# The last two scores of an attention phase: each in a one-bank tile, copied out by VectorE and put under the wide exponential

## The chip, the cores and the metric

One core of a Trainium2 chip. TensorE (PE) multiplies, ScalarE (ACT) computes exponentials, VectorE (DVE) copies and adds, GpSimd (POOL) does small work, SyncE (SP) starts the transfers. The metric is the device time of one execution in microseconds; lower is better. Everything is float32, or float32 as the matmul's faster variant of it (fp32r).

## The reference

Two branches share the input x (2048 tokens, 512 channels) and are mixed by a gate per token. Branch a is softmax attention with 32 heads of 16 channels; branch b is a token-mixing MLP.

```
g = sigmoid((x * gate_w).sum(-1))
q, k, v = split((x @ wqkv), 32 heads of 16)
p = softmax(q k^T / 4);  a = (p v) @ wo
h = layernorm(x);  u = gelu(h^T w1 + b1);  b = (u w2 + b2)^T
out = g * a + (1 - g) * b
```

The exponentials of attention are 32 x 2048 x 2048 numbers. They are the subject of the change.

## The kernel before

**Stages.** Up to about 280 us the kernel loads x, computes the projections, the layer norm and the MLP's first layer. Then comes the attention stage: 128 *phases* in a row (the loop over `p`, 32 groups of two heads and half of the queries, four phases a group). After it, some 35 us of closing projections and stores.

**A phase.** Each phase makes 16 *scores*, numbered 0 to 15. A score is one matmul `kt` x `qt` into one PSUM bank, 128 keys x 512 queries (line 1025). It uses one half of PE's rows, and in the other half a matmul of the MLP's second layer or of a projection runs beside it (`dn`, line 1034; 14 or 12 of them a phase), so the last two or four scores of a phase go as pairs in the two halves. PSUM has eight banks: one is for `dn`, seven for the scores. Scores 0 to 6 take the seven banks; scores 7, 8, 9 reuse the banks of 0, 1, 2; from score 10 on, the banks are reused by tiles of two banks, `t`. Score 9's bank becomes `av` afterwards. The function `shares` says which bank is whose in each phase.

**The exponentials** go three ways, by the tables `EVAC`, `SINGLE` and `TWO`:

- scores 0, 2, 4, 6, 8, 9 (`SINGLE`): ACT takes each from its bank, 512 columns (line 1046);
- pairs (10, 11), (12, 13), (14, 15) (`TWO`): ACT takes two banks at once, 1024 columns (line 991, in `exps`);
- scores 1, 3, 5, 7 (`EVAC`): DVE copies each to the SBUF tile `pe` (line 1042), which frees the bank; when all four are there, ACT takes them at once and in place, 2048 columns (line 1057). Here this is called the *wide exponential*.

**After the scores**, `apply_v` multiplies the exponentials by v (line 921, 64 matmuls of a phase in the trace, four column groups side by side) into the bank `av`, and DVE adds that bank to the sum `ot` (line 943). The wide exponential comes last on ACT, so its scores are *held*: they are applied in the next phase, ahead of that phase's own. Before the change the pair (14, 15) is held with them.

**What sets the order.** The stage is recorded under a manual schedule: each engine runs its instructions in the order in which the code issues them. Waits are semaphores that an instruction raises when it is done. Two things in this order matter for what follows. On ACT a phase is six singles, three pairs, the wide exponential, and then the next phase's singles. And the wide exponential is given a wait beside the one for the copies, with the reason "a later instruction of this engine then waits for one engine alone": it waits for ACT's own instruction `pairs_done[1]`, the second pair of its phase.

```
for x in ([evac] if p < LAST else [evac[:, :2, :], evac[:, 2:, :]]):
    done = nc.scalar.activation(x, x, AF.Exp, scale=SCALE)
tc.add_manual_dep(done.ins, pairs_done[1].ins.name, SYNC, reason=EARLY)
```

On DVE a phase is four copies, then what the plan puts there (a tiny `mark`, casts of weights at line 67, in eight phases the five instructions of a late query projection, lines 67, 68 and 609 to 611), then the addition at line 943.

Of the kernel before, what the change touches and what calls it, by code (L numbers as in the profile page):

```python
# [9 lines left out]
F32 = mybir.dt.float32  # L10
# [13 lines left out]
P = 128  # L24
# [8 lines left out]
NB = 512  # L33
# [27 lines left out]
def gated_mix(ctx: ExitStack, tc: tile.TileContext, a_x, a_wqkv, a_wo, b_w1, b_b1, b_w2, b_b2, gate_w, out):  # L61
# [116 lines left out]
    with tc.tile_pool(name="vp", bufs=1, side="right") as pool:  # L178
# [15 lines left out]
        turns = {}  # L194
# [378 lines left out]
    LAST = NG * PHASES - 1  # L573
# [301 lines left out]

    token, mark = (out_pool.tile([1, 1], F32, name=name, bufs=1) for name in ("token", "mark"))

    EVAC = 1, 3, 5, 7
    SINGLE = 0, 2, 4, 6, 8, 9
    TWO = (10, 11), (12, 13), (14, 15)  # L880
    TURNS = [(0, 2), (4, 6), (8, 9), *TWO]
    HELD = [(1, 3), (5, 7)]

    def shares(n):

# [62 lines left out]
    with tc.manual_schedule(engines=engines):  # L948
        held, fence, turn, spare = [], None, 0, 0
        landed.clear()  # L950

        for p in range(LAST + 1):
            grp, ph = divmod(p, PHASES)
            second = ph % 2
            if ph == 0:
                sums[grp] = ot_pool.tile([P, NB], F32, name="ot")
                latest["clear"] = nc.gpsimd.memset(sums[grp], 0.0)
                at = [[0, 0], [0, 0]]
                if grp + 1 < NG:
                    qt[grp + 1] = load_q(grp + 1)  # L960
            if ph == 1 and grp + 1 < NG:
                kt[grp + 1] = load_k(grp + 1)
            for what, *args in calls.get(p, ()):
                what(*args)
            if not second:
                beside = [step(*args) for step, *args in dense.get(p // 2, ())]
            n_b = len(beside)
            half = slice(0, HALF) if second else slice(HALF, P)

            head = [second if n < n_b else (n - n_b + second * n_b) % 2 for n in range(NSC)]  # L970
            qbs = {}
            order = list(TURNS)
            if ph == 0 and n_b == NSC - 4:
                order[-2:] = (12, 14), (13, 15)
            for a, b in order + HELD:
                if head[a] == head[b]:
                    qbs[a], qbs[b] = 0, 1
                else:
                    zero, one = (a, b) if head[a] == 0 else (b, a)
                    qbs[zero], qbs[one] = turn, 1 - turn  # L980
                    turn = 1 - turn

            swap = ph == PHASES - 1 and p < LAST and n_b == NSC - 2
            if swap:
                order[-2:] = order[:-3:-1]

            def exps(n):
                pt = ptp.tile([P, 2, NB], F32, name="p2", bufs=len(TWO) + 1)
                where = [share[(j - BANKS) % BANKS] for j in (n - 1, n)]
                low = min(where)  # L990
                pairs_done.append(nc.scalar.activation(pt, twos[low, low + 1], AF.Exp, scale=SCALE))  # L991
                for j, k in zip((n - 1, n), where):
                    units[j] = *units[j][:3], pt[:, k - low, :]

            pairs_done = []
            evac = evp.tile([P, len(EVAC), NB], F32, name="pe")
            units = {}
            share = shares(spare)
            pool = regions()
            psum = pool.__enter__()  # L1000
            ones = [psum.tile([P, NB], F32, name=f"s{n}") for n in range(BANKS)]
            for n in range(NSC):
                i, qb = head[n], qbs[n]
                c = at[i][qb]
                at[i][qb] += 1
                if n < TWO[0][0]:
                    if n >= BANKS:
                        ones[share[n - BANKS]] = psum.tile([P, NB], F32, name=f"s{share[n - BANKS]}")
                    s = ones[share[n % BANKS]]
                else:  # L1010
                    if n == TWO[0][0]:
                        pool.__exit__(None, None, None)
                        pool = regions()
                        psum = pool.__enter__()
                        twos = {}
                        for low in range(BANKS):
                            if low == share[2]:
                                av = psum.tile([P, NB], F32, name="av")
                            elif low not in twos:
                                two = psum.tile([P, 2, NB], F32, name=f"t{low}")  # L1020
                                twos[low], twos[low + 1] = two[:, 0, :], two[:, 1, :]
                                twos[low, low + 1] = two
                    s = twos[share[(n - BANKS) % BANKS]]
                rows_i = slice(i * HALF, i * HALF + ROWS)
                nc.tensor.matmul(  # L1025
                    s,
                    kt[grp][rows_i, c * P : (c + 1) * P],
                    qt[grp][rows_i, qb * NB : (qb + 1) * NB],
                    start=True,
                    stop=True,  # L1030
                )
                if n < n_b:
                    ps, a, b, begin, last, done = beside[n]
                    mm = nc.tensor.matmul(ps, a[half], b[half], start=begin and not second, stop=last and bool(second))  # L1034
                    if n == 0 and fence is not None:
                        tc.add_manual_dep(mm.ins, fence.ins.name, SYNC, reason=REASON)
                    if n == n_b - 1:
                        fence = nc.gpsimd.memset(token, 0.0)  # L1038
                        tc.add_manual_dep(fence.ins, mm.ins.name, SYNC, reason=REASON)
                if n in EVAC:  # L1040
                    pt = evac[:, EVAC.index(n), :]
                    nc.vector.tensor_copy(pt, s)  # L1042
                    units[n] = i, c, qb, pt
                elif n in SINGLE:
                    pt = ptp.tile([P, NB], F32, name="p1", bufs=len(SINGLE))
                    nc.scalar.activation(pt, s, AF.Exp, scale=SCALE)  # L1046
                    units[n] = i, c, qb, pt
                else:
                    units[n] = i, c, qb, None
                    if n == TWO[0][1] or n == TWO[1][1] and not swap:  # L1050
                        exps(n)
                    elif n == TWO[2][1]:
                        exps(n)
                        if swap:
                            exps(TWO[1][1])
            for x in ([evac] if p < LAST else [evac[:, :2, :], evac[:, 2:, :]]):
                done = nc.scalar.activation(x, x, AF.Exp, scale=SCALE)  # L1057
            tc.add_manual_dep(done.ins, pairs_done[1].ins.name, SYNC, reason=EARLY)
            evac_done.append(done)
            if n_b and second and beside[-1][-1]:  # L1060
                beside[-1][-1]()
            if p == 0:
                shift_rows(nc.gpsimd, k_bufs[1])
            if p:
                met = nc.vector.memset(mark, 0.0)
                for before in (evac_done[-2], latest["add"], latest["clear"]):
                    tc.add_manual_dep(met.ins, before.ins.name, SYNC, reason=EARLY)
            if second:
                for _ in range(2):
                    if len(ready) < 2:  # L1070
                        split_weight(nc.vector.tensor_copy)
            for what, *args in later.get(p, ()):
                what(*args)

            turns, now_held = ([tuple(units[n] for n in pair) for pair in pairs] for pairs in (order, HELD))
            spare = share[2]
            if p < LAST:
                now_held = now_held + turns[-1:]
                turns = turns[:-1]
            if ph == 0:  # L1080
                if held:
                    apply_v(av, grp - 1, held, final=True)
                    spare = share[3]
                    av = twos[spare]
                apply_v(av, grp, turns)
            elif p < LAST:
                apply_v(av, grp, held + turns, await_loads=ph == PHASES - 1)
            else:
                ot = sums[grp]
                nc.vector.tensor_scalar_max(ot, ot, least[0])  # L1090
                apply_v(av, grp, held + turns + now_held, final=True)
                last_ot = ot
            pool.__exit__(None, None, None)
            held = now_held
            if ph == PHASES - 1:
                assert at == [[NS, NS], [NS, NS]]
# [166 lines left out]
```

## Time and profile before

| what | value |
|---|---|
| median of 3 runs | 1273.06 us (1272.27 to 1273.28) |
| the profiled execution, whole | 1273.23 us |
| its span, first to last instruction | 1271.4 us |
| DVE busy | 685.1 us, 54% of the span |
| POOL busy | 198.9 us, 16% |
| mean granted PE clock | 0.999 |
| first and last wide exponential | start at 284.4 and 1236.0 us |

The times below come from the one profiled execution, whose whole time lies 1.83 us above its span and 0.17 us above the median. In rows of the timeline the first number is the start in us from the start of the span, the second how long the row lasts from the first start to the last end; "x6" is six instructions that follow each other, whose times overlap.

### The profile page before, as it was taken

What the parts mean: (1) busy time and instruction counts of PE and PEld (TensorE: products, weight loads), DVE (VectorE), ACT (ScalarE), POOL (GpSimd) and SP (SyncE); (2) the same over time, 40 slices, a digit from 0 to 9 for tenths busy, and PEclk for the clock granted to TensorE, in tenths of its full rate; (3) what the DMA queues carried; (4) which work ended last, traced back from release to release, by engine and by line L of the source; (5) the groups of instructions that cost most, each with busy time, mean ns of one, the idle gap of its engine ahead of it and who ended that gap; (6) DMA issues with size and microseconds to landing.
All of it is one profiled execution on the core that took longest, in us unless ns stands there. A gap on an engine that the chain in (4) does not pass through costs nothing.

```text
span 1271.4 us, 32690 instructions
## 1 busy us (share of the span) xinstructions
PE 1263.2 (99%) x13342; PEld 827.5 (65%) x13342; DVE 685.1 (54%) x1282; ACT 1076.4 (85%) x1533; POOL 198.9 (16%) x316
## 2 busy tenths in 40 slices
PE   9999999999999999999999999999999999999998
PEld 7888888875666666666566666666666666655556
DVE  5675453176645554555555455554555455456763
ACT  4443343269999999999999999999999999999990
POOL 0220444561011101010110101111111111000000
PEclk9999999999999999999999999999999999999999
DMA  3798443253654443534344443443543443366511
GB/s 132 247 343 328 139 128 100 79 133 114 206 124 102 86 104 77 163 79 97 80 99 101 92 100 74 90 86 77 116 101 63 98 100 60 56 167 184 140 57 70
DMA packets 100555, 152.32 MB, mean 120 GB/s; under 512 B 17109, under 2 KB 56171, under 8 KB 96300
## 3 DMA queue, kind: packets, MB, share of 16 engines
q1 hardware_dynamic: 99820, 149.08, 45.6%
q8 instruction: 108, 1.77, 0.6%
q10 hardware_dynamic: 576, 1.05, 0.2%
q14 instruction: 51, 0.42, 0.1%
HBM read 105.39 MB, written 44.68 MB: 118 GB/s over the span
## 4 chain that ended last, share of the span: by engine, by line
PE 93%; ACT 5%; DMA 0%; DVE 0%; issue 0%; SPq 0%
PE av L921 29%; PE s L1025 21%; PE acc L424 12%; PE t L1025 12%; PE acc L75 8%; PE t L921 5%; PE dn L1034 2%; ACT p L1046 2%; PE pa L1115 2%; ACT p L991 2%; ACT pe L1057 1%; PE acc L199 1%; PE acc L268 0%; DMA x<-in_A_x_dram 0%; PE pa L1145 0%
## 5 line engine op out<-in xcount | busy, mean ns | idle before, releaser
L1046 ACT ACTIVATE p<-s 128x512 f32<-128x512 f32 x768 | 421.8, 863 | 0.1
L991 ACT ACTIVATE p<-t 128x1024 f32<-128x1024 f32 x384 | 404.9, 1341 | 0.0
L1025 PE MATMUL s<-qs,ks 64*128 64x512 f32 x1280 | 329.7, 400 | 0.5 <-ACT p L1046 0.4
L1042 DVE COPY pe<-s 128x512 f32<-128x512 f32 x512 | 318.1, 684 | 4.8 <-PE s L1025 0.6
L921 PE MATMUL av<-p,v 128*32 128x256 f32 x4904 | 288.1, 379 | 0.0
L1025 PEld LDWEIGHTS s<-qs,ks 64*128 64x128 f32 x1280 | 226.1, 184 | 93.5 <-issue 51.9
L1057 ACT ACTIVATE pe<-pe 128x2048 f32<-128x2048 f32 x129 | 286.2, 2222 | 0.0
L943 DVE TENSOR_TENSOR ot<-av,ot 128x512 f32<-128x512 f32 (+2 forms) x140 | 84.8, 606 | 358.0 <-PE av L921 357.7
L921 PEld LDWEIGHTS av<-p,v 128*32 128x32 f32 x4904 | 159.4, 110 | 105.2 <-issue 0.2
L1025 PE MATMUL t<-qs,ks 64*128 64x512 f32 x768 | 189.4, 428 | 0.0
L1034 PE MATMUL dn<-u_hi,w_hi 64*128 64x512 f32 x448 | 182.4, 407 | 0.0
L1034 PE MATMUL dn<-u_lo,w_hi 64*128 64x512 f32 x448 | 182.2, 407 | 0.0
L1034 PE MATMUL dn<-u_hi,w_lo 64*128 64x512 f32 x448 | 182.2, 407 | 0.0
L68 POOL TENSOR_TENSOR w_lo<-w_raw,w_hi 128x512 fp32r<-128x512 f32 (+1 forms) x128 | 152.9, 1201 | 121.4 <-ACT w_hi L67 99.8
L1025 PEld LDWEIGHTS t<-qs,ks 64*128 64x128 f32 x768 | 96.3, 184 | 87.6 <-ACT p L1046 87.5
L1038 POOL MEMSET token<- 1x1 f32 x128 | 12.0, 94 | 829.5 <-PE dn L1034 776.8
L921 PE MATMUL av<-pe,v 128*32 128x256 f32 x2048 | 137.3, 385 | 0.1
L67 ACT CAST w_hi<-w_raw 128x512 fp32r<-128x512 f32 (+1 forms) x67 | 38.0, 570 | 82.7 <-PE acc L424 63.1
L921 PEld LDWEIGHTS av<-pe,v 128*32 128x32 f32 x2048 | 53.5, 109 | 60.9 <-ACT p L1046 38.4
L424 PE MATMUL acc<-h_hi,w_hi 128*128 128x512 f32 x224 | 87.9, 392 | 0.0
L424 PE MATMUL acc<-h_hi,w_lo 128*128 128x512 f32 x224 | 87.8, 392 | 0.0
L424 PE MATMUL acc<-h_lo,w_hi 128*128 128x512 f32 x224 | 87.8, 392 | 0.0
(161 smaller groups left out, 1446.4 us busy)
## 6 DMA issues: line engine op xcount, KB each, us to landing
w_raw<-in_B_w_dram SPq DMA_DIRECT2D x96, 256.0 KB
ks<-kp SPq DMA_DIRECT2D x192, 128.0 KB
qs<-qp SPq DMA_DIRECT2D x256, 64.0 KB
kp<-pc SPq DMA_DIRECT2D x16, 512.0 KB
qp<-pc SPq DMA_DIRECT2D x8, 768.0 KB
qp<-row SPq DMA_DIRECT2D x24, 256.0 KB
v<-v SPq DMA_DIRECT2D x4, 1088.0 KB
x<-in_A_x_dram SPq DMA_DIRECT2D x16, 256.0 KB
```

The source lines that it names most:

```text
L67: copy(hi, src)
L68: return sub(lo, src, hi.bitcast(F32), ALU.subtract)
L75: nc.tensor.matmul(ps, a, b, start=start and n == 0, stop=stop and n == last)
L424: nc.tensor.matmul(p, a, b, start=first and k == 0, stop=last and k == 2)
L921: mm = nc.tensor.matmul(av[32 * j : 32 * (j + 1), i * QC : (i + 1) * QC], vb[b][:, v_at : v_at + 32], pt[:, h * QC : (h + 1) * QC], start= ...
L943: latest["add"] = nc.vector.tensor_tensor(x, y, x, ALU.add)
L991: pairs_done.append(nc.scalar.activation(pt, twos[low, low + 1], AF.Exp, scale=SCALE))
L1025: nc.tensor.matmul(s, kt[grp][rows_i, c * P : (c + 1) * P], qt[grp][rows_i, qb * NB : (qb + 1) * NB], start=True, stop=True,)
L1034: mm = nc.tensor.matmul(ps, a[half], b[half], start=begin and not second, stop=last and bool(second))
L1042: nc.vector.tensor_copy(pt, s)
L1046: nc.scalar.activation(pt, s, AF.Exp, scale=SCALE)
L1057: done = nc.scalar.activation(x, x, AF.Exp, scale=SCALE)
```

## The change

The scores 14 and 15 leave `TWO` and join `EVAC`: each has a one-bank tile `u`, DVE copies it to `pe`, which is now six tiles wide, and the wide exponential covers 3072 columns. They are held for the next phase as before. With two pairs left, the special orders of the pairs (`order`, `swap`) go, and which score lies in which half of PE's rows is set by `alone` and `in_turn`. The line with `pairs_done[1]` stays as it is.

```diff
-    EVAC = 1, 3, 5, 7
+    EVAC = 1, 3, 5, 7, 14, 15
     SINGLE = 0, 2, 4, 6, 8, 9
-    TWO = (10, 11), (12, 13), (14, 15)
+    TWO = (10, 11), (12, 13)
     TURNS = [(0, 2), (4, 6), (8, 9), *TWO]
-    HELD = [(1, 3), (5, 7)]
+    HELD = [(1, 3), (5, 7), (14, 15)]
...
-            head = [second if n < n_b else (n - n_b + second * n_b) % 2 for n in range(NSC)]
+            alone = NSC - (NSC - n_b) // 2
+            head = [second if n < alone else 1 - second for n in range(NSC)]
+            in_turn = list(range(n_b)) + [n for pair in zip(range(n_b, alone), range(alone, NSC)) for n in pair]
...
-            for a, b in order + HELD:
+            for a, b in TURNS + HELD:
...
-                pt = ptp.tile([P, 2, NB], F32, name="p2", bufs=len(TWO) + 1)
+                pt = ptp.tile([P, 2, NB], F32, name="p2", bufs=len(TWO))
...
-            for n in range(NSC):
+            for n in in_turn:
...
+                            elif low in share[:2]:
+                                twos[low] = psum.tile([P, NB], F32, name=f"u{low}")
...
-                    if n == TWO[0][1] or n == TWO[1][1] and not swap:
+                    if n in (TWO[0][1], TWO[1][1]):
                         exps(n)
-                    elif n == TWO[2][1]:
-                        exps(n)
-                        if swap:
-                            exps(TWO[1][1])
...
-            if p < LAST:
-                now_held = now_held + turns[-1:]
-                turns = turns[:-1]
```

ACT's order in one phase, before (lines 1046, 991, 1057; `s`, `t` are PSUM tiles, `p1`, `p2`, `pe` the exponentials):

```order
L1046 ACTIVATE p1_9029<-s3_9023 128x512 [waits PE_49]
L1046 ACTIVATE p1_9036<-s2_9022 128x512 [waits PE_49]
L1046 ACTIVATE p1_9043<-s6_9026 128x512 [waits PE_49]
L1046 ACTIVATE p1_9050<-s0_9020 128x512 [waits PE_49]
L1046 ACTIVATE p1_9059<-s4_9056 128x512 [waits PE_49]
L1046 ACTIVATE p1_9064<-s2_9061 128x512 [waits PE_49]
L991 ACTIVATE p2_9078<-t5_9073 128x1024 [waits PE_49]
L991 ACTIVATE p2_9085<-t0_9070 128x1024 [waits PE_49]
L991 ACTIVATE p2_9089<-t3_9072 128x1024 [waits PE_49]
L1057 ACTIVATE pe_9016<-pe_9016 128x2048 [waits DVE_49,Activation_49]
```

The same phase after the change (the lines are now 1043, 986, 1050):

```order
L1043 ACTIVATE p1_9081<-s3_9075 128x512 [waits PE_49]
L1043 ACTIVATE p1_9088<-s2_9074 128x512 [waits PE_49]
L1043 ACTIVATE p1_9095<-s6_9078 128x512 [waits PE_49]
L1043 ACTIVATE p1_9102<-s0_9072 128x512 [waits PE_49]
L1043 ACTIVATE p1_9111<-s4_9108 128x512 [waits PE_49]
L1043 ACTIVATE p1_9116<-s2_9113 128x512 [waits PE_49]
L986 ACTIVATE p2_9131<-t5_9126 128x1024 [waits PE_49]
L986 ACTIVATE p2_9138<-t0_9122 128x1024 [waits PE_49]
L1050 ACTIVATE pe_9068<-pe_9068 128x3072 [waits DVE_49,Activation_49]
```

The third pair is gone, and the wide exponential stands right behind the second pair, which is the instruction of its own engine that it waits for. Before, the third pair stood between the two.

DVE's order around a phase, before (lines 1042 copies, 1065 `mark`, 67 casts, 943 addition):

```order
L1042 COPY pe_9632<-s2_9638 128x512 [waits PE_49]
L1042 COPY pe_9632<-s3_9639 128x512 [waits PE_49]
L1042 COPY pe_9632<-s6_9642 128x512 [waits PE_49]
L1042 COPY pe_9632<-s1_9668 128x512 [waits PE_49]
L1065 MEMSET mark_2618 1x1 [waits DVE_49,Activation_49]
L67 CAST w_hi_9709<-w_raw_8769 128x512
L67 CAST w_hi_9713<-w_raw_9014 128x256 [waits PE_49]
L943 TENSOR_TENSOR ot_9490<-av_9686,ot_9490 128x512 [waits PE_49]
```

And after the change (lines 1039, 1058, 67, 943):

```order
L1039 COPY pe_9689<-s2_9695 128x512 [waits PE_49]
L1039 COPY pe_9689<-s3_9696 128x512 [waits PE_49]
L1039 COPY pe_9689<-s6_9699 128x512 [waits PE_49]
L1039 COPY pe_9689<-s1_9725 128x512 [waits PE_49]
L1039 COPY pe_9689<-u1_9744 128x512 [waits PE_49]
L1039 COPY pe_9689<-u2_9745 128x512 [waits PE_49]
L1058 MEMSET mark_2618 1x1 [waits DVE_49,Activation_49]
L67 CAST w_hi_9767<-w_raw_8819 128x512
L67 CAST w_hi_9771<-w_raw_9066 128x256
L943 TENSOR_TENSOR ot_9547<-av_9743,ot_9547 128x512 [waits PE_49]
```

The two further copies stand ahead of everything else that the phase gives DVE.

More of the change, by code (lines that the diff above doesn't have):

```diff
@@ L968, in gated_mix @@
             half = slice(0, HALF) if second else slice(HALF, P)
-            head = [second if n < n_b else (n - n_b + second * n_b) % 2 for n in range(NSC)]
+            alone = NSC - (NSC - n_b) // 2
+            head = [second if n < alone else 1 - second for n in range(NSC)]
+            in_turn = list(range(n_b)) + [n for pair in zip(range(n_b, alone), range(alone, NSC)) for n in pair]
             qbs = {}
-            order = list(TURNS)
-            if ph == 0 and n_b == NSC - 4:
-                order[-2:] = (12, 14), (13, 15)
-            for a, b in order + HELD:
+            for a, b in TURNS + HELD:
                 if head[a] == head[b]:
@@ L981, in gated_mix @@
                     turn = 1 - turn
-            swap = ph == PHASES - 1 and p < LAST and n_b == NSC - 2
-            if swap:
-                order[-2:] = order[:-3:-1]
             def exps(n):
-                pt = ptp.tile([P, 2, NB], F32, name="p2", bufs=len(TWO) + 1)
+                pt = ptp.tile([P, 2, NB], F32, name="p2", bufs=len(TWO))
                 where = [share[(j - BANKS) % BANKS] for j in (n - 1, n)]
@@ L1049, in gated_mix @@
                     units[n] = i, c, qb, None
-                    if n == TWO[0][1] or n == TWO[1][1] and not swap:
+                    if n in (TWO[0][1], TWO[1][1]):
                         exps(n)
-                    elif n == TWO[2][1]:
-                        exps(n)
-                        if swap:
-                            exps(TWO[1][1])
             for x in ([evac] if p < LAST else [evac[:, :2, :], evac[:, 2:, :]]):
@@ L1073, in gated_mix @@
                 what(*args)
-            turns, now_held = ([tuple(units[n] for n in pair) for pair in pairs] for pairs in (order, HELD))
+            turns, now_held = ([tuple(units[n] for n in pair) for pair in pairs] for pairs in (TURNS, HELD))
             spare = share[2]
-            if p < LAST:
-                now_held = now_held + turns[-1:]
-                turns = turns[:-1]
             if ph == 0:
```

## The prediction

> **What bounds the kernel now.** I read the page first, then busy time by stretches, then ACT's timeline of a few phases, and last PE and DVE around the end of a phase's scores.
>
> ```profile
> span 1271.4 us, 32690 instructions
> PE 93%; ACT 5%; DMA 0%; DVE 0%; issue 0%; SPq 0%
> L1046 ACT ACTIVATE p<-s 128x512 f32<-128x512 f32 x768 | 421.8, 863 | 0.1
> L991 ACT ACTIVATE p<-t 128x1024 f32<-128x1024 f32 x384 | 404.9, 1341 | 0.0
> L1042 DVE COPY pe<-s 128x512 f32<-128x512 f32 x512 | 318.1, 684 | 4.8 <-PE s L1025 0.6
> L1057 ACT ACTIVATE pe<-pe 128x2048 f32<-128x2048 f32 x129 | 286.2, 2222 | 0.0
> ...
> core 0: us, PE busy (x) PEld busy (x) DVE busy (x) ACT busy (x) POOL busy (x), PEclk, DMA share, GB/s
> 400.00:500.00 100.00, 100.00 (x1244) 60.97 (x1244) 51.43 (x104) 100.00 (x137) 10.48 (x24) 1.00 0.42 91
> 700.00:800.00 100.00, 100.00 (x1252) 60.94 (x1254) 54.27 (x110) 100.00 (x136) 10.47 (x24) 1.00 0.41 88
> ...
> PEld t L1025 <- ACT p L1046: 87.5, 383, 0.3
> PEld av L921 <- ACT p L1046: 38.4, 127, 0.3
> ```
>
> The chain puts PE at 93%, but PE's busy time is modelled. Of PE and ACT, both at 100.00 of 100 us, PE is the one that waits: its weight loads stood 87.5 + 38.4 us waiting for singles, in some 510 places, four a phase, and ACT waits for nothing that shows. So I look at ACT's phases, in two places.
>
> ```profile
> 704.01 2.25 ACT L1057 ACTIVATE pe<-pe 128x2048 f32<-128x2048 f32 x1
> 705.89 3.31 ACT L1046 ACTIVATE p<-s 128x512 f32<-128x512 f32 x6
> 708.77 3.17 ACT L991 ACTIVATE p<-t 128x1024 f32<-128x1024 f32 x3
> 711.49 2.25 ACT L1057 ACTIVATE pe<-pe 128x2048 f32<-128x2048 f32 x1
> 713.38 3.31 ACT L1046 ACTIVATE p<-s 128x512 f32<-128x512 f32 x6
> ...
> 1222.13 3.17 ACT L1046 ACTIVATE p<-s 128x512 f32<-128x512 f32 x6
> 1225.00 3.05 ACT L991 ACTIVATE p<-t 128x1024 f32<-128x1024 f32 x3
> 1227.71 2.13 ACT L1057 ACTIVATE pe<-pe 128x2048 f32<-128x2048 f32 x1
> 1229.51 3.27 ACT L1046 ACTIVATE p<-s 128x512 f32<-128x512 f32 x6
> ```
>
> A phase is 711.49 - 704.01 = 7.48 us, and (1227.71 - 284.42) / 126 = 7.49 over the stage. The starts give the steps of an ACT that is not held up: six singles 1225.00 - 1222.13 = 2.87, so 0.478 each; three pairs 2.71, so 0.903 each; the wide exponential 1229.51 - 1227.71 = 1.80. Together that is 7.38. Yet a single lasts 0.86 us and a pair 1.34: an instruction starts while the one before is still being written. By ends the phase is full: the wide one ends at 706.26, the singles at 709.20, the pairs at 711.94, the next wide one at 713.74, in steps of 2.94, 2.74 and 1.80, which make 7.48. So **ACT's write side paces the stage**; the starts run up to 0.3 us ahead of it, and then wait.
>
> **How long a pair lasts when nothing is piled up behind it** decides this case.
>
> ```profile
> 284.42 1.99 ACT L1057 ACTIVATE pe<-pe 128x2048 f32<-128x2048 f32 x1
> 283.51 1.10 ACT L991 ACTIVATE p<-t 128x1024 f32<-128x1024 f32 x1
> 1187.48 2.25 ACT L991 ACTIVATE p<-t 128x1024 f32<-128x1024 f32 x2
> 1189.49 1.16 ACT L991 ACTIVATE p<-t 128x1024 f32<-128x1024 f32 x1
> L991 ACT ACTIVATE p<-t x384: 1067/1350/1376, 281.7 to 1234.2; 128x1024 f32<-128x1024 f32 x192
> ```
>
> In the first phase of the stage the pairs last 1.07 to 1.10 us, in the steady phases 1.35 (the median). A pair that had to wait some 0.2 us (it starts at 1189.49, two steps of 0.903 after 1187.48 would be 1189.29) lasts 1.16 and not 1.35. So a wait costs ACT's ends little as long as it only eats this lead. The lead grows by (1.10 - 1.07) / 2, about 0.013 us, from one instruction to the next.
>
> **The change part by part.** Let T be the start of a phase's first single.
>
> *The third pair goes, the wide exponential grows.* The pair's step, 0.903, is removed. 512 more columns cost 0.903 - 0.478 = 0.425 us, so the wide one's step becomes 1.80 + 0.85 = 2.65. That alone gains 0.05 us a phase by starts, since one instruction's fixed part is saved.
>
> *The wait for the second pair becomes real.* The code ties the wide exponential to `pairs_done[1]`. Before, a third pair started in between; the second, one step after 708.77 and 1.35 long, was over by 711.03, ahead of the wide one's start at 711.49, so the wait was free. Now the awaited pair stands right in front. What a wait for the instruction just ahead costs, ACT does not show before the change; DVE does:
>
> ```profile
> 167.01 0.43 DVE L437 TENSOR_SCALAR gs<-gs 128x512 f32<-128x512 f32 x1
> 167.47 0.69 DVE L438 TENSOR_TENSOR gs<-gs,gu 128x512 f32<-128x512 f32 x1
> 706.12 2.48 DVE L1042 COPY pe<-s 128x512 f32<-128x512 f32 x4
> ```
>
> Line 438 reads what line 437 wrote, and starts 0.03 us after its end. Copies that need nothing of each other start 0.60 apart ((2.48 - 0.68) / 3) while each lasts 0.68. So the wide exponential will start when the second pair has ended and 0.03 later, not 0.903 after the pair's start. The pair's time from start to end is bounded by 1.07 and 1.35 from the rows above. I take 1.11: the wait stops ACT once a phase, so the lead begins anew at the wide exponential, and the second pair is the eighth instruction after it. A fresh pair is about 1.02 (1.07 was the fourth in an unbroken row, 4 x 0.013 less), and seven steps of 0.013 make 1.11.
>
> The new phase is 2.87 + 0.90 + 1.11 + 0.03 + 2.65 = 7.56 to 7.57 us, against 7.48: **+0.09 a phase**, x 126 = 11 us. Queued behind the waiting instruction on ACT are the next phase's six singles, for which PE waits to get banks and `av`.
>
> *Does PE or DVE take over?* PE:
>
> ```profile
> 708.84 0.42 PE L1025 MATMUL t<-qs,ks 64*128 64x512 f32 x2
> 709.25 1.07 PE L921 MATMUL av<-pe,v 128*32 128x256 f32 x16
> 712.84 0.50 PE L1025 MATMUL s<-qs,ks 64*128 64x512 f32 x1
> ```
>
> From ACT's last single (ends 709.20) to the next first score (713.34) PE needs 4.14 us; the singles' ends come at T + 3.31 or, with less lead, 3.06. PE's own loop is thus 7.45 at most and 7.2 with the smaller lead, under 7.57: PE gains slack. Its matmuls stay the same in number, and no wait is added there but score 14's on a copy.
>
> DVE gets two more copies a phase, 2 x 0.60 = 1.2 us of its queue; it is 51 to 54% busy, so there is room on the mean. Scores 14 and 15 are made by 709.26, T + 3.37, and 0.25 earlier with the smaller lead. Two copies (0.60 + 0.68, 0.04 to start) end at T + 4.69 at the latest, more likely T + 4.44. The second pair ends at T + 2.87 + 0.90 + 1.11 = T + 4.88. **The copies are covered by 0.2 to 0.4 us**; without that cover every further 0.1 us costs 13 us over the stage. What DVE does behind them moves 1.2 us later. In most phases that is little, but not in these:
>
> ```profile
> 633.79 0.69 DVE L67 CAST row<-dn 128x512 fp32r<-128x512 f32 x1
> 637.14 0.06 DVE L1065 MEMSET mark<- 1x1 f32 x1
> 638.19 0.69 DVE L943 TENSOR_TENSOR ot<-av,ot 128x512 f32<-128x512 f32 x1 [0.99 <-PE av L921]
> 638.81 2.48 DVE L1042 COPY pe<-s 128x512 f32<-128x512 f32 x4
> L611 DVE TENSOR_REDUCE z<-dn x8: 682/683/684, 337.3 to 756.2; 128x1 f32<-128x512 f32 x8
> ```
>
> Here a late query's chain takes 3.4 us and DVE idled 0.99 before the addition. Pushed back by two copies that end at T + 4.4, it ends at about T + 7.75, the addition's step of 0.62 makes T + 8.4, and the next phase's first copy, wanted at about T + 7.8 (0.23 after the first single), is 0.5 us late. Score 8 needs that copy's bank, and ACT wants score 8 four singles after the first; most of the 0.5 is absorbed there, and I leave 0.2 to 0.3 in each of the 8 phases, 2 us, and 1 to 2 us for the few phases of the last 100 us in which DVE splits rows of 1024 columns. Bounds: 0, or the whole 0.5 in each of them and in as many others, 8 us.
>
> *The rest at nothing:* the new order of heads and the dropped `swap` leave as many matmuls, and PE has slack to hide them; where the held pair's halves differ, the addition at line 943 splits in two parts once a group at most, on DVE before the next copies.
>
> **Sum:** 1273.2 (the profiled execution) + 11 + 3.5 = 1287.7, say 1288; the median of the runs shown stands 0.2 lower.
>
> **The rivals.**
>
> *The copies end last.* If DVE reaches scores 14 and 15 more than 0.2 to 0.4 us late in most phases, the wide exponential waits for them. At 0.4 past the second pair's end: +0.4 x 126 = 50 us more, at 0.1: 13, so 1300 to 1338. For it: the addition and the new copies share one queue. Against it: before the copies DVE stands idle, 0.99 us even in the row above. 10%.
>
> *The lead does not shrink.* If the awaited pair lasts 1.35 as now, the phase is 7.81 and the time 1273 + 0.33 x 126 + 3 = 1318. Against it stand the 1.16 after a wait and the 1.07 at the start of the stage. 7%.
>
> *The wait is free: the other side.* If an instruction may start beside the one of its own engine that it waits for, only the saved step is left: 0.05 to 0.06 x 126 = 6 to 8 us less, 1265 to 1267, and with the 3.5 us of DVE's late phases up to 1271. It decides if the wide exponential's start comes 0.90 after the second pair's. For it: ACT paces the stage. Against it: line 438's row. 9%.
>
> The Trainium skill, VectorE: DVE Perf Modes, section "The DRAIN you can't avoid", reports that eight DVE copies took equally long with a semaphore after each and with one after the last, so that a semaphore costs nothing extra. By that rule this rival holds; the trace does not bear it out here, with 0.03 us after the end where a wait is and 0.08 us before it where none is.
>
> The same skill's Perfetto Trace Analysis, section "Optimizing Scalar/DVE Operations", gives a fixed 51 ns for ScalarE on PSUM and says that grouping into larger operations helps a saturated engine. The trace agrees on the size (0.478 - 0.425 = 0.053), and by that rule alone the time would be about 1267.
>
> *The change isn't what it says:* the order above shows it is; no chance given.
>
> **How the numbers follow.** My forecast has 72%, the copies 10%, the full lead 7%, the free wait 9%, and 2% are left for anything else. The forecast's own range is 1281 to 1297: 1.07 for the pair and no late phases on one side, 8 us of late phases on the other. To hold 8 in 10 it reaches a little towards the rivals: 1277 to 1303. The three runs lie 1 us apart; 0.2% (2.5 us) is what can be told from no change. Faster by more: most of the free wait, 6%. Within: 4%. Slower: 90%.
>
> **What would show each step.** In ACT's timeline of the changed kernel the wide exponential starts 1.1 to 1.2 us after the second pair's start and the phases are 7.55 to 7.6 long; pairs last about 1.1 and singles 0.6 to 0.7. PE's waits for singles shrink. Two copies more per phase end before the second pair does. In the eight late-query phases a phase is 0.2 to 0.3 longer. I am wrong if the wide exponential starts with DVE's last copy, or 0.90 after the pair.

## The result, and the profile after

The changed kernel takes **1290.21 us** (median of 4 runs, 1289.91 to 1290.58) against 1272.90 (4 runs, 1272.27 to 1273.28): 1.0137 times the time before, with a 95% interval of 1.0119 to 1.0154. It is slower by 17.3 us; the profiled spans, 1288.5 and 1271.4, differ by 17.1. The forecast was 1288, in a range of 1277 to 1303.

The lines of the page of the changed kernel that answer to those of before (span, the costliest groups: busy us and mean ns, then idle time ahead), and two rows of the table of waits (total us, times, longest):

```profile
span 1288.5 us, 32655 instructions
L1043 ACT ACTIVATE p<-s 128x512 f32<-128x512 f32 x768 | 388.4, 605 | 5.0 <-PE s L1022 2.8
L1050 ACT ACTIVATE pe<-pe 128x3072 f32<-128x3072 f32 x129 | 354.5, 2749 | 5.1 <-DVE mark L1058 1.0
L986 ACT ACTIVATE p<-t 128x1024 f32<-128x1024 f32 x256 | 254.3, 1076 | 0.0
...
PEld t L1022 <- ACT p L1043: 53.3, 220, 0.4
PEld av L921 <- ACT p L1043: 36.4, 119, 0.4
```

On the mean a single became 0.26 us shorter (605 ns, was 863) and a pair 0.27 shorter (1076, was 1341), and yet the kernel is slower. Busy time alone would have told a gain: that of ACT's three lines was 421.8 + 404.9 + 286.2 = 1113 us and is 997. The length of an ACT row says here how much is piled up ahead of its end, not what it costs: from the first single's start to the first pair's it is still 2.86, 2.88 before. What sets the time is seen in the timeline of ACT (start, how long the row lasts, count), in two steady phases, with PE's first score of the second:

```profile
713.73 3.02 ACT L1043 ACTIVATE p<-s 128x512 f32<-128x512 f32 x6
716.59 1.99 ACT L986 ACTIVATE p<-t 128x1024 f32<-128x1024 f32 x2
718.61 2.77 ACT L1050 ACTIVATE pe<-pe 128x3072 f32<-128x3072 f32 x1
721.28 3.02 ACT L1043 ACTIVATE p<-s 128x512 f32<-128x512 f32 x6
...
726.16 2.77 ACT L1050 ACTIVATE pe<-pe 128x3072 f32<-128x3072 f32 x1
...
720.39 0.49 PE L1022 MATMUL s<-qs,ks 64*128 64x512 f32 x1
```

The pairs start 0.90 apart, so the second starts at 717.49; the row ends at 716.59 + 1.99 = 718.58, and the wide exponential starts at 718.61: 0.03 after the end of the instruction that it waits for, and 1.12 after its start. The steps by starts are 2.86 (six singles), 0.90, 1.12 and 2.67, together 7.55 to 7.56, where a phase took 7.48 before. Over 126 phases this is 10 us of the 17. PE did not become the bound: its first score is done at 720.88 and ACT takes it at 721.28, 0.40 later. Before the change ACT took it 0.04 after its end (713.34 and 713.38 in the rows of the prediction), so there a phase's first single stood for PE, which no row shows as idle time, since the wide exponential was still being written. PE's waits for singles fell from 126 to 90 us.

In DVE's timeline the two new copies are done in time. They end at 718.19, which is 0.39 ahead of the end of the pair (over the stage the median is 0.47):

```profile
716.90 1.29 DVE L1039 COPY pe<-u 128x512 f32<-128x512 f32 x2 [0.59 <-PE u L1022]
```

The other 7 us lie in a few long phases. By the starts of the wide exponential, the eight late-query phases take 8.00 to 8.10 each (0.45 more than their neighbours, 3.7 in all), three others 8.27 to 8.33 (2.2), and near the end one 7.79 and one 9.04 (1.7). With the first phases of the stage (two of 8.07 to 8.08) what lies off the median adds up to 8.4 us. Before the change it was 0.8, from two first phases of 7.90; the phases of 7.70 near its end stand beside others of 7.38 and leave the mean at 7.48. Of these 7.5 us more, 0.9 is made up for by a stage that starts earlier. A late-query phase on ACT, DVE and PE, from three pieces of the timeline:

```profile
703.05 2.77 ACT L1050 ACTIVATE pe<-pe 128x3072 f32<-128x3072 f32 x1
705.72 0.58 ACT L1043 ACTIVATE p<-s 128x512 f32<-128x512 f32 x1
706.63 2.56 ACT L1043 ACTIVATE p<-s 128x512 f32<-128x512 f32 x5 [0.33 <-PE s L1022]
...
711.05 2.77 ACT L1050 ACTIVATE pe<-pe 128x3072 f32<-128x3072 f32 x1
...
705.03 0.68 DVE L611 TENSOR_REDUCE z<-dn 128x1 f32<-128x512 f32 x1
705.64 0.69 DVE L943 TENSOR_TENSOR ot<-av,ot 128x512 f32<-128x512 f32 x1
...
704.84 0.50 PE L1022 MATMUL s<-qs,ks 64*128 64x512 f32 x1
705.86 0.47 PE L1031 MATMUL dn<-u_hi,w_hi 64*128 64x512 f32 x1 [0.53 <-DVE mark L1058]
```

PE makes the first score at 704.84, and then a `dn` matmul stands in its queue until 705.86, with all the other scores of the phase behind it. Line 611, the last instruction that reads the old `dn` bank, ends at 705.71. The `mark` that the row names is a tiny instruction that ends just behind it. ACT gets score 0 in time and stops 0.33 for the next one. In a late-query phase before the change the same two rows, the last reader of `dn` and the first `dn` matmul, were:

```profile
636.51 0.68 DVE L611 TENSOR_REDUCE z<-dn 128x1 f32<-128x512 f32 x1
...
638.05 0.50 PE L1034 MATMUL dn<-u_hi,w_hi 64*128 64x512 f32 x1
```

There the reader was done at 637.19, 0.86 before the matmul. Two copies ahead of it, 1.2 us, are more than that. One of the three others, on the same engines:

```profile
960.91 2.77 ACT L1050 ACTIVATE pe<-pe 128x3072 f32<-128x3072 f32 x1
...
965.46 1.69 ACT L1043 ACTIVATE p<-s 128x512 f32<-128x512 f32 x3 [0.33 <-PE dn L1031]
...
969.24 2.77 ACT L1050 ACTIVATE pe<-pe 128x3072 f32<-128x3072 f32 x1 [0.26 <-DVE mark L1058]
...
964.20 0.68 DVE L943 TENSOR_TENSOR ot<-av,ot 128x512 f32<-128x512 f32 x1
...
964.93 0.49 PE L1022 MATMUL s<-qs,ks 64*128 64x512 f32 x1 [0.59 <-DVE ot L943]
```

Here the plan has DVE do three instructions of line 1066 first, from 960.87 to 964.28. PE waits 0.59 for a bank until the addition of line 943, which follows them, has read `av`, ACT waits 0.33 for PE, and at the end of the phase the copies of 14 and 15 come last for once: the wide exponential stands 0.26 more, until DVE is done.

### The profile page after: what moved, and what is told of

It is laid out like the page before. It is cut to its first block, busy times and chain, and to the rows that moved or that the text cites. A ratio compares the mean times of both kernels' runs of the same rounds, so it can differ in the third digit from the quotient of the medians.

```text
span 1288.5 us, 32655 instructions
## 1 busy us (share of the span) xinstructions
PE 1273.4 (99%) x13342; PEld 846.5 (66%) x13342; DVE 854.2 (66%) x1547; ACT 1084.4 (84%) x1405; POOL 199.2 (15%) x316
## 4 chain that ended last, share of the span: by engine, by line
PE 92%; DVE 4%; ACT 2%; DMA 1%; issue 1%; SPq 0%; DVEq 0%; ACTq 0%
PE av L921 26%; PE s L1022 19%; PE acc L424 12%; PE t L1022 9%; PE acc L75 8%; PE dn L1031 6%; PE t L921 5%; PE u L1022 3%; PE pa L1105 2%; DVE pe L1039 1%; ACT pe L1050 1%; PE acc L199 1%; ACT p L1043 1%; DVE row L610 0%; DVE row L68 0%
## 5 line engine op out<-in xcount | busy, mean ns | idle before, releaser
L1043 ACT ACTIVATE p<-s 128x512 f32<-128x512 f32 x768 | 388.4, 605 | 5.0 <-PE s L1022 2.8
L1050 ACT ACTIVATE pe<-pe 128x3072 f32<-128x3072 f32 x129 | 354.5, 2749 | 5.1 <-DVE mark L1058 1.0
L986 ACT ACTIVATE p<-t 128x1024 f32<-128x1024 f32 x256 | 254.3, 1076 | 0.0
L921 PE MATMUL av<-p,v 128*32 128x256 f32 x3880 | 227.2, 379 | 0.0
L1039 DVE COPY pe<-u 128x512 f32<-128x512 f32 x256 | 165.0, 686 | 85.5 <-PE u L1022 73.8
L921 PE MATMUL av<-pe,v 128*32 128x256 f32 x3072 | 192.5, 383 | 0.1
L921 PEld LDWEIGHTS av<-p,v 128*32 128x32 f32 x3880 | 126.0, 110 | 83.3 <-issue 0.2
L1022 PE MATMUL t<-qs,ks 64*128 64x512 f32 x512 | 157.1, 423 | 0.0
L921 PEld LDWEIGHTS av<-pe,v 128*32 128x32 f32 x3072 | 86.7, 109 | 83.2 <-ACT p L1043 36.4
L1022 PEld LDWEIGHTS t<-qs,ks 64*128 64x128 f32 x512 | 79.3, 184 | 55.5 <-ACT p L1043 53.3
```

The costliest lines, as they stand in the source:

```text
L921: mm = nc.tensor.matmul(av[32 * j : 32 * (j + 1), i * QC : (i + 1) * QC], vb[b][:, v_at : v_at + 32], pt[:, h * QC : (h + 1) * QC], start= ...
L1022: nc.tensor.matmul(s, kt[grp][rows_i, c * P : (c + 1) * P], qt[grp][rows_i, qb * NB : (qb + 1) * NB], start=True, stop=True,)
```

## The experiments

Two theories were to be told apart for the steady phases. By the prediction's, what costs is the wait for the instruction just ahead on the same engine, and the rest of the change is a small gain. Its rivals say that the copies end last, or that six copies and a wider exponential are dearer in themselves.

**The same kernel, but waiting for the first pair.** Only the name of the instruction that the wide exponential waits for is changed; another pair then stands between.

```diff
-            tc.add_manual_dep(done.ins, pairs_done[1].ins.name, SYNC, reason=EARLY)
+            tc.add_manual_dep(done.ins, pairs_done[0].ins.name, SYNC, reason=EARLY)
```

> The changed kernel, but the wide exponential waits for the first pair of its phase (pairs_done[0]) and no more for the second, which stands right in front of it. If the wait for the instruction just ahead is what made it slower, the wide exponential starts 0.90 to 1.0 us after the second pair instead of 1.11, a steady phase falls from 7.56 to 7.41 to 7.47 us, and the time to 1272 to 1281 (the late phases of VectorE stay). If the copies of scores 14 and 15 set the start, or if ACT's own columns do, nothing changes: 1289 to 1291.

It took 1280.13 us (1279.80 to 1280.90; ratio to before 1.0059, 1.0042 to 1.0076), 10 us less than the change. Its ACT timeline, first a late-query phase, then two plain ones, and DVE's last reader of `dn` in the late-query phase:

```profile
697.74 2.90 ACT L1050 ACTIVATE pe<-pe 128x3072 f32<-128x3072 f32 x1
...
701.88 2.56 ACT L1043 ACTIVATE p<-s 128x512 f32<-128x512 f32 x5 [0.66 <-PE s L1022]
...
706.11 2.81 ACT L1050 ACTIVATE pe<-pe 128x3072 f32<-128x3072 f32 x1
...
716.18 3.09 ACT L1043 ACTIVATE p<-s 128x512 f32<-128x512 f32 x6
719.04 2.06 ACT L986 ACTIVATE p<-t 128x1024 f32<-128x1024 f32 x2
720.84 2.91 ACT L1050 ACTIVATE pe<-pe 128x3072 f32<-128x3072 f32 x1
723.50 3.19 ACT L1043 ACTIVATE p<-s 128x512 f32<-128x512 f32 x6
726.36 2.16 ACT L986 ACTIVATE p<-t 128x1024 f32<-128x1024 f32 x2
728.16 3.00 ACT L1050 ACTIVATE pe<-pe 128x3072 f32<-128x3072 f32 x1
...
700.28 0.68 DVE L611 TENSOR_REDUCE z<-dn 128x1 f32<-128x512 f32 x1
```

The second pair starts at 719.94 and the wide exponential 0.90 later, while the pair is still being written (to 721.10). The median phase is 7.42. So the wait is worth 0.14 a phase, 17 to 18 us over the stage, and without it the change wins 0.06 a phase, 8 us: one fixed part of an instruction, as the sum had it. The kernel is slower than before all the same, since what lies off the median adds up to 16 us in place of 8: the late-query phases are 8.35 now (697.74 to 706.11 is 8.37), with ACT stopped 0.66, and the last fifteen are mostly 7.56. In the late-query phase the reader of `dn` ends 3.22 after the wide exponential's start (700.96 - 697.74), where it ended 2.66 after it in the change: ACT without its wait has run closer to DVE, and the same chain stops it for longer. The copies have no cover left here: in most phases the wide exponential starts 0.09 after the last of them. What makes the last fifteen longer was not tried.

**The kernel before, waiting for its third pair.** The opposite edit: nothing of the change, only a wait for the instruction just ahead.

```diff
-            tc.add_manual_dep(done.ins, pairs_done[1].ins.name, SYNC, reason=EARLY)
+            tc.add_manual_dep(done.ins, pairs_done[2].ins.name, SYNC, reason=EARLY)
```

> The kernel before, with the wide exponential waiting for the third pair of its phase (pairs_done[2]), the one just ahead of it, instead of the second; nothing else. If that wait costs what the forecast says, the wide exponential starts 1.11 to 1.15 us after the third pair instead of 0.90, a phase is 2.87 + 1.81 + 1.14 + 1.80 = 7.62 to 7.65 us, and the time 1290 to 1295. If an own-engine wait is free, 1273; if the pair still lasted 1.35, 1318 or more.

It took 1289.98 us (1289.97 to 1290.92; ratio 1.0137, 1.0120 to 1.0154). Its ACT timeline:

```profile
716.20 2.90 ACT L991 ACTIVATE p<-t 128x1024 f32<-128x1024 f32 x3
719.13 1.92 ACT L1057 ACTIVATE pe<-pe 128x2048 f32<-128x2048 f32 x1
...
726.75 1.92 ACT L1057 ACTIVATE pe<-pe 128x2048 f32<-128x2048 f32 x1
```

The third pair starts at 716.20 + 1.81 = 718.01 and ends at 719.10, the wide exponential starts 0.03 later, and the phase is 7.62: 0.14 more than before, 18 us over 126 phases, with no copy added and no long phase beyond those of before. The wait by itself, in either kernel, has the same price. That settles the steady part: neither the copies nor the width of the exponential had to do with it. The rule that the prediction weighed, from the Trainium skill, VectorE: DVE Perf Modes, section "The DRAIN you can't avoid", that a semaphore costs nothing extra, does not carry over to this wait.

**The late-query phases: the last reader of `dn` one place earlier.** In the changed kernel the reduction, which reads the bank, is put ahead of the instruction that reads only SBUF.

```diff
             nc.vector.tensor_scalar(most_k, ps, most[:, b : b + 1], None, ALU.mult)
-            nc.vector.scalar_tensor_tensor(most_k.bitcast(F32R), most_k, -1.0, most_k, ALU.mult, ALU.max)
             nc.vector.tensor_reduce(qmax[:, b, n : n + 1], ps, axis=AX.X, op=ALU.max, apply_absolute_value=True)
+            nc.vector.scalar_tensor_tensor(most_k.bitcast(F32R), most_k, -1.0, most_k, ALU.mult, ALU.max)
```

> The changed kernel, with the late query's reduction of the bank dn (line 611) moved ahead of the step that does not read dn (line 610), so the bank is free 0.61 us earlier in eight phases; VectorE's work is the same. If those phases are long because PE's next dn matmul waits for that reduction, they fall from 8.00 to 7.6 to 7.75 us, 2 to 3.5 us in all, to 1287 to 1288. If they are long because the next phase's first copy is late in VectorE's queue, they stay at 8.00 and the time at 1290.

It took 1286.65 us (1286.32 to 1286.74; ratio to before 1.0108, 1.0091 to 1.0124), 3.6 less than the change. The same phase as above, on ACT and DVE:

```profile
700.35 2.77 ACT L1050 ACTIVATE pe<-pe 128x3072 f32<-128x3072 f32 x1
703.02 3.02 ACT L1043 ACTIVATE p<-s 128x512 f32<-128x512 f32 x6
...
707.90 2.77 ACT L1050 ACTIVATE pe<-pe 128x3072 f32<-128x3072 f32 x1
...
701.61 0.68 DVE L610 TENSOR_REDUCE z<-dn 128x1 f32<-128x512 f32 x1
702.20 0.68 DVE L611 SCALAR_TENSOR_TENSOR row<-row 128x512 fp32r<-128x512 f32 x1
702.81 0.68 DVE L943 TENSOR_TENSOR ot<-av,ot 128x512 f32<-128x512 f32 x1
...
703.41 2.47 DVE L1039 COPY pe<-s 128x512 f32<-128x512 f32 x4
```

The phase is 7.55, as long as its neighbours, though DVE does the same five instructions. The reduction ends 1.94 after the start of the wide exponential (702.29 - 700.35), 2.66 before the edit; the addition starts 2.46 after it, 2.59 before the edit, since the reduction needs nothing of the instruction now ahead of it. What held the eight phases up was the bank `dn`, and not the late first copy that the prediction named: that copy still starts 0.39 after the phase's first single (703.41 against 703.02), where the prediction's rows had 0.23, and the phase is as short as the others. (One phase, the fourth of the stage, became 8.05 with this edit; there the wide exponential stands 0.26 for the copies. Why only with this edit stays open.)

**Both edits together.** The wait for the first pair and the earlier reduction:

> The changed kernel with both edits: the wide exponential waits for the first pair, and the late query's reduction of dn comes before the step that does not read dn. If the eight late-query phases (8.35 us there) are long mostly because of the bank dn, they fall to 7.7 to 7.9 and the time from 1280.1 to 1275 to 1277. If ACT without its stop is held up by VectorE's queue there instead, they stay over 8.1 and the time at 1278 to 1280.

It took 1277.14 us (1276.30 to 1277.27; ratio 1.0032, 1.0020 to 1.0044), 3 us under the first experiment. Its steady phase is 7.41, but the late-query phases are still 8.06, which lies between the two outcomes that were expected and meets neither. In one of them the wide exponential starts 0.40 later than two pair steps allow, with DVE named ahead of it:

```profile
522.46 1.95 ACT L986 ACTIVATE p<-t 128x1024 f32<-128x1024 f32 x2
524.66 2.77 ACT L1050 ACTIVATE pe<-pe 128x3072 f32<-128x3072 f32 x1 [0.26 <-DVE mark L1058]
...
523.28 1.29 DVE L1039 COPY pe<-u 128x512 f32<-128x512 f32 x2 [0.59 <-PE u L1022]
```

The copies end at 524.57, later than the pair itself (524.41). So the first edit's gain is partly given back in another place. This is 0.40 of the 0.65 by which the phase is longer than its neighbours; the rest was not followed.

**The cover of the copies.** The changed kernel with score 14 copied twice to the same place, which makes the last copy later and leaves the result as it is:

```diff
                     nc.vector.tensor_copy(pt, s)
+                    if n == 14:
+                        nc.vector.tensor_copy(pt, s)
```

> The changed kernel, with score 14 copied twice in every phase, so that the last copy ends 0.60 us later. If the second pair's end sets the start of the wide exponential and the copies have a cover of 0.39 us, a phase grows by 0.2 to 0.3 us, to 7.76 to 7.86, and the time to 1315 to 1330. If the copies already set the start, a phase grows by the whole 0.60 and the time to 1366.

One run took 1337.57 us, above the 1315 to 1330 that were expected. DVE and ACT in a steady phase:

```profile
738.00 0.69 DVE L1039 COPY pe<-u 128x512 f32<-128x512 f32 x1 [1.06 <-PE u L1022]
738.72 0.69 DVE L1041 COPY pe<-u 128x512 f32<-128x512 f32 x1
739.33 0.68 DVE L1039 COPY pe<-u 128x512 f32<-128x512 f32 x1
...
732.24 2.77 ACT L1052 ACTIVATE pe<-pe 128x3072 f32<-128x3072 f32 x1 [0.56 <-DVE mark L1060]
...
740.10 2.77 ACT L1052 ACTIVATE pe<-pe 128x3072 f32<-128x3072 f32 x1 [0.34 <-DVE pe L1039]
```

The repeated copy writes what the one ahead wrote, so it waits for it and starts 0.03 after its end, at 738.72; the next, which needs neither, starts 0.61 after that. The last copy is thus 0.72 later than it would be, and with a cover of 0.39 the phase should grow by 0.33: the median is 7.87, so 0.31. The wide exponential now waits for DVE. That is 39 us of the 47 over the change; the other 8 are again the long phases, 9.08 for the late-query ones. So "the copies end last" is a mechanism of this kernel; the change alone stays clear of it in its steady phases, by 0.39 in the one shown.

**A choice by phase.** Where a phase has 14 matmuls beside its scores, is none of the first four, and has no planned work on DVE, it goes as changed, with the wait for the first pair. Every other phase keeps the heads of before and gives (14, 15) to ACT as a third pair, written beside the four copies into the same six-wide tile, with the wide exponential over 2048 columns and the wait for the second of three pairs.

```diff
+            light = n_b == NSC - 2 and p >= 4 and not later.get(p)
...
-                pt = ptp.tile([P, 2, NB], F32, name="p2", bufs=len(TWO))
+                pt = whole[:, 4:, :] if n == 15 else ptp.tile([P, 2, NB], F32, name="p2", bufs=len(TWO))
...
-            evac = evp.tile([P, len(EVAC), NB], F32, name="pe")
+            whole = evp.tile([P, len(EVAC), NB], F32, name="pe")
+            evac = whole if light else whole[:, :4, :]
...
-                if n in EVAC:
+                if n in EVAC[: 6 if light else 4]:
...
-            tc.add_manual_dep(done.ins, pairs_done[0].ins.name, SYNC, reason=EARLY)
+            tc.add_manual_dep(done.ins, pairs_done[0 if light else 1].ins.name, SYNC, reason=EARLY)
```

> Both forms, chosen by phase: the change with the wait on the first pair in the light phases (14 matmuls beside the scores, no extra work planned on VectorE, not the first four), some 80 of 128; in the others ACT takes scores 14 and 15 as a third pair again, written into the same tile pe, and the wide exponential covers 2048 columns. If the gain of a light phase is 7.48 - 7.41 = 0.07 us and the losses of the variant with the first pair all lie in the phases in which VectorE is late, the time is 1273 - 80 x 0.07 = 1267 to 1269. If the copies disturb the light phases too, 1273 or more.

It took **1268.12 us** (5 runs, 1267.68 to 1268.36; ratio to before 0.9961, 0.9948 to 0.9975): faster than both kernels, by 4.8 and 22.1 us. ACT's timeline, a phase of the old kind and two of the new:

```profile
574.60 2.23 ACT L1053 ACTIVATE pe<-pe 128x2048 f32<-128x2048 f32 x1
...
581.22 3.02 ACT L1053 ACTIVATE pe<-pe 128x3072 f32<-128x3072 f32 x1
...
586.83 2.19 ACT L988 ACTIVATE p<-t 128x1024 f32<-128x1024 f32 x2
588.65 3.01 ACT L1053 ACTIVATE pe<-pe 128x3072 f32<-128x3072 f32 x1
```

In the new kind the wide exponential starts 0.92 after the second pair, and the phase is 588.65 - 581.22 = 7.43. There are 76 such phases, and 76 x 0.06 is 4.6 us, the gain. None of the late-query phases is long any more. (Where the kind changes, the wide exponential stands in another place of its phase, so that two of its steps are 8.32 and 6.65; together they are two phases of 7.48.)

## Why the prediction was right, point by point

**The wait becomes real: right.** Predicted: the wide exponential starts 1.11 + 0.03 after the second pair's start. It starts 1.12 after; the pair lasts 1.085, at the low end of the bounds of 1.07 to 1.35. That a wait shortens the pile-up, the point on which 1288 or 1318 hung, is seen in every row: pairs of 1.08 and singles of 0.60. The second experiment shows the wait alone to cost 17 us in the kernel before, the first that the change without it has a phase of 7.42. (The lead's growth worked out in the prediction, (1.10 - 1.07) / 2, is 0.015 and not 0.013; the 1.11 comes out with either.)

**The step that is saved: right.** The wide exponential's step came out as 2.67 (predicted 2.65), the removed pair's as 0.90. Without the wait the phase gains 0.06, predicted 0.05. The Trainium skill's Perfetto Trace Analysis, section "Optimizing Scalar/DVE Operations", says that larger operations can help a saturated engine. The traces agree on the size of that gain. The 1267 that followed from that rule alone were missed by 23 us in the change, because grouping also took away the instruction that had stood between the wide exponential and the one it waits for, and because of the long phases.

**+0.09 a phase, 11 us: a little high.** 0.08, and 10 us.

**PE gains slack, the copies are covered: right.** ACT takes PE's first score 0.40 after it is done, 0.04 before the change, and PE's waits for singles went from 126 to 90 us. The prediction's "7.45 at most" for PE's own loop left out those 0.04; with them the loop was as long as the phase before, 7.48 to 7.49, and PE had no slack then. The copies end 0.39 ahead of the pair in the row shown and 0.47 on the median, at or above the top of the 0.2 to 0.4 given, and the fifth experiment turns that cover into time.

**DVE's late phases, 3.5 us: mis-sized, and for the eight phases put down to the wrong wait.** All long phases together cost 7.5 us more than before, twice the term and within the bound of 8 that was given: 3.7 in the eight late-query ones, 2.2 in three others, which the bound allowed for but the term did not, 1.7 near the end, where 1 to 2 were predicted, less the 0.8 of before, plus some 0.7 from the start of the stage and small differences. The prediction reckoned that a late-query phase makes the next phase's first copy late by 0.5, that most of this is absorbed, and that 0.2 to 0.3 is left. What it missed is that DVE's chain does not only stand ahead of the copies: it is also the reader of the bank `dn`, and PE's queue holds a `dn` matmul right behind the first score. Pushed back by two copies, the last reader ends after that matmul's turn, and nothing absorbs this, since all further scores are behind it. Each phase lost 0.45, and moving that one reader by one place gave it back. In the three other phases the late addition holds a bank of PE, as the rows of one of them show; this was read, not tried.

**The sum: right, with some luck.** The wait's term was 1 us too high and DVE's 4 too low, and a stage that starts 0.9 earlier took back part of the latter. The inner range of 1281 to 1297 does not follow from the terms named for it, which give about 1279 (1.07 for the pair, no late phases) and 1292 (8 us of late phases); the time lies within either.

## What to carry to other kernels

In both kernels tried here, ACT's wait for an instruction of its own was free while another instruction stood between the two, and cost 0.14 us a phase when none did. When a change removes the one between, look again at every wait that is named by its place in a list: this one line made 10 of the 17 us, and turned 0.06 us won in a plain phase into 0.08 lost. Count ACT's steps from start to start and from end to end, never by the length of its rows, which fell by a fifth to nearly a third while the kernel got slower. And before giving an idle engine more work ahead of its queue, ask for every bank which it reads later who stands waiting to write it: a change that pays in the plain phases and costs in the busy ones can be chosen phase by phase.

## What the runs showed of the hardware that was not expected

The wait for the instruction just ahead costs the same in both kernels: 0.14 us a phase between 7.42 and 7.56, and between 7.48 and 7.62. At the wide exponential itself it is more, 1.12 - 0.90 = 0.22. Some 0.07 of it comes back, most of it in the wide exponential's step, which is 2.67 with the wait and 2.70 to 2.73 in steady phases without it: with the wait, the first single no longer stands for PE.

After a stop ACT can run by its starts for a few phases before its ends hold it back. In the kernel that waits for the first pair, a long phase is followed by three of 7.32 to 7.40 (behind a late-query phase one of 7.40 to 7.45 comes first), and then they are about 7.41. Its rows show the pile growing meanwhile: the six singles last 3.09 and then 3.19, the pairs 2.06 and then 2.16, the wide one 2.91 and then 3.00. That is about 0.1 us for each phase of nine instructions, close to the 0.013 from one instruction to the next that the prediction read from the start of the stage. So the ends go on at the same pace: the wide exponential that starts at 728.16 does so 7.32 after the one before, and ends 7.41 after it. By this the phases behind a stop win a part of it back, some 0.2 to 0.3 us. What then holds the starts back runs through PE: in every steady phase of the kernel before, and of this one, the first single starts 0.04 after PE's first score ends, and that score ends 4.14 after the end of the previous phase's last single.
